# Spectral filter and gated layer on one core: the first stage's folded row in another layout, its last sums taken from VectorE to TensorE in ten of sixteen tiles

## Chip, core and metric

One NeuronCore of a Trainium2 chip runs one program. The time is that of the device for one execution, in microseconds; the kernel before took 716.36 us, the median of 3 runs (715.77 to 716.48). Lower is better.

## What is computed

`x` has 2048 rows (the sequence) of 640 features, in float32. Cut to what matters:

```python
h  = x + irfft2(rfft2(layernorm(x)) * (w_r + 1j * w_i))     # over both axes
z  = layernorm(h)
h2 = h + ((z @ w_gate) * (z @ w_up)) @ w_down               # 640 -> 1728 -> 640
```

`layernorm` takes the mean and the variance of each row, with no weights. All of the Fourier transforms are matrix products with tables of cosines and sines, which the host makes once.

## The kernel before

The 2048 rows lie in 16 tiles of 128 partitions. The forward transform along the rows is split in 128 x 16: **the first stage**, which is all that the change touches, multiplies each tile from the left with a 128x128 table `cct` of cosines and sines; the second stage then does the 640 features (`d_mm`), the other factor of the rows (`s2_mm`), the filter (`filt`), and the way back. After it come the second layernorm, and the gated layer as a long run of matrix products with the weights (a Strassen scheme in three passes of a rounded format).

In the first stage each tile is first *folded*, because a cosine is even about a point and a sine is odd: the 640 features become sums and differences of mirrored features, and half of the multiplications fall away. For tile `t`:

- **Statistics.** Mean and variance of the row. For some tiles VectorE does it (`bn_stats` twice, `bn_aggr`: L133, L134, L135), for those in `ON_ACT` ScalarE (two passes with an accumulator: L148, L149). Then the inverse root, for one, two or four tiles at a time: a square root on ScalarE (L158), and four tiny VectorE instructions, each of which needs the one before (L159 to L162). These four come in iterations 1, 5, 9 and 13 (and 3), zipped between the tile's fold instructions.
- **First fold.** `odd` subtracts mirrored features, for 2 x 160 outputs (L182; on GpSimd for tiles 0 to 6, on VectorE from tile 7 = `AHEAD` on). `even` adds them and takes twice the mean off, for 2 x 161 outputs (L192, one VectorE instruction).
- **Second fold**, within the same line of `even`: L196 adds the two halves for the 33 + 33 features for which TensorE will not do it, L197 subtracts them for 2 x 160.
- **Scaled table.** The inverse root belongs to the rows of the tile, which are summed over; so `scale_c` multiplies it into the table, `CR[t] = cct * r` (L214 on ScalarE for tile 0, L216 on VectorE for the others). Four buffers turn round.
- **Matrix products** (`s1_mm`). The folded tile is the stationary operand, the scaled table (128 columns) the moving one. Four blocks of 128 outputs go to one PSUM bank (`im`): the first two take two products each, over the two halves, so that TensorE does the sum of the second fold there (L208), the other two take one each, from the differences. The remaining 33 + 31 even and 64 odd features make one more product, into a bank of their own (L209). A float32 product is two hardware matmuls, so a tile is 14.
- **Out of PSUM.** ScalarE copies the four blocks (`s1_main`, L227) and the rest (`s1_rest`, L222). The bank of the four blocks has two buffers, so tile `t` waits for L227 of tile `t - 2`.

Each engine works off its own list in order. The order is written by hand: iteration `t` of the loop emits, for ScalarE, L222 of tile `t - 1`, its share of statistics, in some iterations the square root, L227 of tile `t - 1`; for VectorE, `odd` (from tile 7 on), the fold of tile `t` zipped with what `dve[t]` holds, its share of statistics, and the scaled table of tile `t + 1`; for TensorE, the products of tile `t`. Waits between instructions, also between two VectorE instructions of which one reads or overwrites what the other wrote, are put in by the framework, by the address range that each access spans.

After the last tile ScalarE copies its bank in two halves, `rest_split` (L231, L232) makes the rounded pairs, and `d_mm(0)` starts (L83, names `im<-tab,s` and `re<-tab,s`).

Of the kernel before, what the change touches and what calls it, by code (L numbers as in the profile page):

```python
# [14 lines left out]
OP = mybir.AluOpType  # L15

P = 128
S, D, NF, FF = 2048, 640, 321, 1728
NT = S // P
# [4 lines left out]
FOFF = (0, 160, 353, 514)  # L24
NR = 4
AHEAD = 7
ON_ACT = (1, 4, 10, 14)
EPS = 1e-5


def view(t, offset, dims):
    return bass.AP(tensor=t.tensor, offset=t.offset + offset, ap=[list(t.ap[0])] + [list(d) for d in dims])
# [6 lines left out]
def zipped(main, side):  # L39
    n = len(main)  # L40
    for i, f in enumerate(main):
        f()
        for h in side[i * len(side) // n:(i + 1) * len(side) // n]:
            h()
# [3 lines left out]
def tile_spectral_glu(ctx: ExitStack, tc: tile.TileContext, x, wf, wgu, wlast, wdown, wdlast,  # L48
                      cc, ci, fmain, frem, imain, irem, mm, out):
    nc = tc.nc  # L50
# [6 lines left out]
    tt, act = nc.vector.tensor_tensor, nc.scalar.activation  # L57
# [9 lines left out]
    def bank(tag, bufs=2):  # L67
        return pools["a"].tile([P, 512], F32, tag=tag, name=tag, bufs=bufs)
# [23 lines left out]
    XP = [keep.tile([P, D + 1], F32, name=f"x{t}") for t in range(NT)]  # L92
# [72 lines left out]
    SC = {}  # L165

    def front(ts):
        n = len(ts)
        r = small.tile([P, n], F32, tag="r", name="r")
        junk = [fold[:, o:o + D] for o in (NR * 1026, NR * 1026 + D)]  # L170
        m2, ve, fs = moments(ts, junk * 2 if ts[0] in ON_ACT else None)
        for i, t in enumerate(ts):
            SC[t] = r[:, i:i + 1], m2[:, i:i + 1]
        return fs, inverse_root(ve, r, n)

    def folded(t):
        o = t % NR * 1026
        return fold[:, o:o + 642], fold[:, o + 642:o + 1026]

    def odd(t, engine):  # L180
        f = folded(t)[0]
        engine.tensor_tensor(view(f, 0, [[160, 2], [1, 160]]), view(XP[t], 1, [[320, 2], [1, 160]]),  # L182
                             view(XP[t], 639, [[-320, 2], [-1, 160]]), op=OP.subtract)

    def even(t):
        f, j = folded(t)

        def both(n):
            return view(f, 0, [[320, 2], [1, n]]), view(f, 160, [[321, 2], [1, n]])

        return [
            lambda: nc.vector.scalar_tensor_tensor(view(f, 320, [[161, 2], [1, 161]]),  # L192
                                                   view(XP[t], 0, [[320, 2], [1, 161]]), SC[t][1],
                                                   view(XP[t], 640, [[-320, 2], [-1, 161]]),
                                                   op0=OP.subtract, op1=OP.add),
            lambda: tt(view(j, 33, [[-33, 2], [1, 33]]), *both(33), op=OP.add),  # L196
            lambda: tt(view(j, 64, [[1, 2], [2, 160]]), *both(160), op=OP.subtract),  # L197
        ]

    PS1, CR = {}, {}  # L200

    def s1_mm(t):
        pm, pr = PS1[t] = bank("im"), bank("ir2" if t % 2 else "im2", 1)
        (f, j), c = folded(t), CR[t]
        sums = [(f[:, o:o + P], f[:, o + n:o + n + P]) for o, n in ((31, 160), (353, 161))]
        for k, ls in enumerate((*sums, (view(j, 128, [[2, P]]),), (view(j, 129, [[2, P]]),))):
            for n, l in enumerate(ls):
                nc.tensor.matmul(pm[:, k * P:(k + 1) * P], l, c, start=n == 0, stop=n == len(ls) - 1)  # L208
        nc.tensor.matmul(pr[:, 0:P], j[:, 0:P], c, start=True, stop=True)  # L209

    def scale_c(t):
        CR[t] = crs[t % 4]
        if t == 0:
            act(CR[t], cct, AF.Copy, scale=SC[t][0])  # L214
        else:
            nc.vector.tensor_scalar(CR[t], cct, SC[t][0], None, op0=OP.mult)  # L216
# [4 lines left out]
    def s1_rest(t):  # L221
        act(at(rest, t), PS1[t][1][:, 0:P].rearrange("p (g m) -> p g m", g=32), AF.Copy)  # L222

    def s1_main(t):
        n = 4 if t < NT - 1 else 2
        for c in range(0, 4, n):
            act(view(s1, 4 * t + 2048 * c, [[2048, n], [64, 32], [1, 4]]),  # L227
                PS1[t][0][:, c * P:(c + n) * P].rearrange("p (c g m) -> p c g m", c=n, g=32), AF.Copy)
# [4 lines left out]

    banks("a", "pone")
    dve, acts, stats = ([[] for _ in range(NT)] for _ in range(3))
    post = {}

    warm = wk([P, P], "warm")
    nc.vector.memset(warm, 0.0)
# [7 lines left out]
    for first, n, a, b in ((2, 2, 0, 0), (4, 2, 0, 1), (6, 4, 1, 4), (10, 4, 2, 7), (14, 2, 8, 11)):  # L247
        fs, cs = front(range(first, first + n))
        if first in ON_ACT:
            for k, f in enumerate(fs[:-1]):  # L250
                acts[a + k * (b - a + 1) // (2 * n)].append(f)
            dve[b + 1].append(fs[-1])
        else:
            for k, f in enumerate(fs):
                stats[min(b, a + k // 3 * (b - a + 1) // n)].append(f)
        post[first - 2] = cs[0]
        dve[first - 1] += cs[1:]
    odd(0, nc.gpsimd)
    for t in range(NT):
        if t == 1:  # L260
            nc.gpsimd.dma_start(frt, frem)
        if t >= 1:
            s1_rest(t - 1)
            for f in acts[t]:
                f()
            if t >= AHEAD:
                odd(t, nc.vector)
            zipped(even(t), dve[t])
        else:
            e0 = even(0)  # L270
            for f in e0[:1] + c0 + e0[1:] + f1:
                f()
        if t + 2 < AHEAD:
            nc.gpsimd.tensor_copy(small.tile([P, 1], F32, tag="hold", name="hold"), folded(t)[1][:, 383:384])
            for k in (1, 2) if t == 0 else (t + 2,):
                odd(k, nc.gpsimd)
        if t >= 1:
            for f in stats[t]:
                f()
            if t in post:  # L280
                post[t]()
            s1_main(t - 1)
        else:
            scale_c(0)
            for f in c1[:1] + acts[0]:
                f()
            zipped(stats[0], c1[1:])
        if t + 1 < NT:
            scale_c(t + 1)
        if t == 0:  # L290
            post[t]()
        s1_mm(t)
    s1_main(NT - 1)
    s1_rest(NT - 1)
# [221 lines left out]
    def scale_shift(ts, junk, total=None):  # L516
        n = len(ts)
        r = small.tile([P, n], F32, tag="r", name="r")
        b = small.tile([P, n], F32, tag="b", name="b")
        m2, ve, fs = moments(ts, junk, total)  # L520
        cs = inverse_root(ve, r, n)
        cs.append(lambda: nc.vector.scalar_tensor_tensor(b, m2, -0.5, r, op0=OP.mult, op1=OP.mult))
        for i, t in enumerate(ts):
            SC[t] = r[:, i:i + 1], b[:, i:i + 1]
        return fs, cs
# [99 lines left out]
    for p in range(4):  # L625
        ts, t0 = (2 * p, 2 * p + 1), 2 * p + 2
        fs, cs = scale_shift(ts, [scrap] * 2, total[:, ts[0]:ts[0] + 2])
# [218 lines left out]
    for n, (blk, p) in enumerate(steps):  # L846
        if p == 6:
            s13, s12 = count % 3, (count + 1) % 3
            if blk == 0:
                load_raw(0)  # L850
                copies, sums, high, low = prep(0, blk, nc.vector)
# [26 lines left out]
            else:  # L878
                copies, sums, high, low = prep(0, blk)
# [41 lines left out]
            if blk == 0:  # L921
                fs, cs = scale_shift(range(8, 16), None)
# [5 lines left out]
        for ci in range(2):  # L928
            c = 2 * p + ci
# [28 lines left out]
def tables():  # L958
# [3 lines left out]
    for u in range(1, 64):  # L962
        a = 2 * np.pi * ((u * n2) % 128) / 128
# [12 lines left out]
    even = fr % 2 == 0  # L976

    def rows(kind, ds):
        r = np.zeros((len(ds), 2, NQ))
        for i, d in enumerate(ds):  # L980
            half = 0.5 if d == 160 or (d == 0 and kind[0] == "e") else 1.0
            if kind[0] == "e":
                r[i, 0, :NF] = np.where(even == (kind == "ee"), cs(fr, d) * half, 0)
            else:
                r[i, 1, :NF] = np.where(even == (kind == "oe"), -sn(fr, d) * half, 0)
        return r

    main = [rows(*a) for a in (("oe", np.arange(32, 160)), ("ee", np.arange(33, 161)),
                               ("os", np.arange(33, 161)), ("eo", np.arange(32, 160)))]
    cut = [(1, 0), (0, 0), (1, 160), (0, 160)]  # L990
    fmain = np.concatenate([a[:, b, o:o + w] for a, (b, o), w in zip(main, cut, FW)], 1)
    frem = np.concatenate([rows("ee", np.arange(33)), rows("oe", np.arange(1, 32)),
                           np.stack([rows("os", np.arange(1, 33)), rows("eo", np.arange(32))], 1).reshape(64, 2, NQ)])

    m = np.zeros((32, 128, 128), np.float64)
# [3 lines left out]
    for u in range(64):  # L999
        g, v = divmod(u, 2)  # L1000
        for pm in range(2):
            k = (u if pm == 0 else (128 - u if u else 64)) + 128 * r16
# [3 lines left out]
            for s in range(2):  # L1006
                pr = r16 * 4 + v * 2 + s
                if u == 0:
                    a = 1.0 if s == pm else 0.0
                else:  # L1010
                    a = 1.0 if s == 0 else (-1j if pm == 0 else 1j)
                w = (a * tw).T
# [4 lines left out]
                w = np.conj(a * tw) / (S * D)  # L1017
# [16 lines left out]
    for i, f in enumerate(fr):  # L1034
        a = 1.0 if f in (0, 320) else 2.0
        o = slice(0, 161) if f % 2 == 0 else slice(161, 322)
# [48 lines left out]
```

## Time and profile before

| | |
|---|---|
| median of 3 runs | 716.36 us |
| the profiled execution | 716.83 us |
| its span, first to last instruction | 715.0 us |
| TensorE clock granted | 0.999 |
| busy over the span: TensorE / VectorE / ScalarE / GpSimd | 98% / 65% / 36% / 40% |
| first stage: first VectorE work on a tile | 4.79 us |
| last tile's bank begins to leave PSUM | 44.08 us |
| first matmul of the second stage | 44.51 us |

How to read it: the profiled execution takes 1.83 us more than its span, and lies 0.47 us above the median. Lines are those of the kernel before. In the rows of a timeline the first number is the start in us from the beginning of the span, the second the duration of one instruction, or of a merged group from its first start to its last end; behind it stand engine, line, operation, out<-in, shapes and count, and in brackets how long the engine stood idle before and what ended that. PE is TensorE's matmuls, PEld its weight loads, DVE VectorE, ACT ScalarE, POOL GpSimd. The end of a matmul is modelled, and matmuls overlap, so their starts are what counts.

### The profile page before, as it was taken

What the parts mean: (1) busy time and instruction counts of PE and PEld (TensorE: products, weight loads), DVE (VectorE), ACT (ScalarE), POOL (GpSimd) and SP (SyncE); (2) the same over time, 40 slices, a digit from 0 to 9 for tenths busy, and PEclk for the clock granted to TensorE, in tenths of its full rate; (3) what the DMA queues carried; (4) which work ended last, traced back from release to release, by engine and by line L of the source; (5) the groups of instructions that cost most, each with busy time, mean ns of one, the idle gap of its engine ahead of it and who ended that gap; (6) DMA issues with size and microseconds to landing.
All of it is one profiled execution on the core that took longest, in us unless ns stands there. A gap on an engine that the chain in (4) does not pass through costs nothing.

```text
span 715.0 us, 10103 instructions
## 1 busy us (share of the span) xinstructions
PE 698.9 (98%) x3898; PEld 620.4 (87%) x3898; DVE 464.1 (65%) x808; ACT 254.6 (36%) x486; POOL 283.1 (40%) x263
## 2 busy tenths in 40 slices
PE   8899998999999999999999999999999999999998
PEld 7789998877788888989898989888888989898987
DVE  7978887897876656565555558565645555555454
ACT  6766665365532212222222255341222222222210
POOL 3101114331074645454554624055445355464600
PEclk9999999999999999999999999999999999999999
DMA  9406764000121212121211212301202121110203
GB/s 335 175 12 200 231 207 150 1 1 29 46 75 38 74 37 74 38 74 38 74 38 51 75 42 111 124 24 38 74 37 75 38 74 37 60 52 6 69 1 148
DMA packets 20928, 55.06 MB, mean 77 GB/s; under 512 B 2320, under 2 KB 6928, under 8 KB 20880
## 3 DMA queue, kind: packets, MB, share of 16 engines
q1 hardware_dynamic: 20304, 52.70, 21.3%
q0 software_dynamic: 288, 1.48, 0.6%
q8 instruction: 31, 0.51, 0.3%
q10 hardware_dynamic: 288, 0.23, 0.1%
q14 instruction: 17, 0.14, 0.1%
HBM read 49.16 MB, written 5.24 MB: 76 GB/s over the span
## 4 chain that ended last, share of the span: by engine, by line
PE 84%; DVE 11%; ACT 2%; issue 1%; DMA 1%; DVEq 0%; ACTq 0%
PE e L83 45%; PE y L83 27%; PE re L83 2%; PE im L83 2%; PE u L341 2%; PE eo L83 2%; PE im L383 1%; DVE x L512 1%; DVE fold L197 1%; DVE fold L192 1%; PE ir L383 1%; DMA raw<-in_wgu_dram 1%; ACT zt L529 1%; DVE x L514 1%; DMA x<-in_x_dram 1%
## 5 line engine op out<-in xcount | busy, mean ns | idle before, releaser
L83 PE MATMUL e<-xt,wst 128*128 128x512 f32 x864 | 206.8, 390 | 0.0
L83 PE MATMUL y<-wd,ht 128*128 128x320 f32 x1312 | 201.4, 310 | 1.2 <-DVE x L512 1.1
L83 PEld LDWEIGHTS y<-wd,ht 128*128 128x128 f32 x1312 | 195.3, 188 | 5.7 <-DVE x L512 2.7
L83 PEld LDWEIGHTS e<-xt,wst 128*128 128x128 f32 x864 | 160.7, 188 | 31.7
L512 DVE TENSOR_TENSOR x<-y,x 128x640 f32<-128x640 f32 x119 | 97.6, 821 | 70.4 <-PE y L83 70.1
L709 POOL TENSOR_TENSOR wst<-raw,wst 128x1024 fp32r<-128x1024 f32 x23 | 55.6, 2416 | 154.1 <-ACT wst L708 154.1
L725 POOL TENSOR_TENSOR wst<-raw,wst 128x896 fp32r<-128x896 f32 (+1 forms) x46 | 65.0, 1436 | 22.4 <-ACT wst L720 22.4
L468 POOL TENSOR_TENSOR wd<-draw,wd 128x640 fp32r<-128x640 f32 x28 | 44.9, 1627 | 72.1 <-ACT wd L467 72.1
L83 PE MATMUL e<-t,wst 128*128 128x512 f32 x288 | 73.2, 389 | 0.0
L821 ACT ACTIVATE ht<-e 128x512 fp32r<-128x512 f32 x24 | 14.4, 598 | 153.1 <-DVE e L820 153.1
L83 PEld LDWEIGHTS e<-t,wst 128*128 128x128 f32 x288 | 54.0, 188 | 11.7 <-DVE ht L660 0.5
L835 ACT ACTIVATE ht<-e 128x512 fp32r<-128x512 f32 x24 | 14.4, 598 | 114.0 <-DVE e L834 114.0
L83 PE MATMUL e<-xt,wdir 128*128 128x512 f32 x180 | 42.1, 392 | 1.2 <-DVE ht L664 1.2
L83 PEld LDWEIGHTS e<-xt,wdir 128*128 128x128 f32 x180 | 33.5, 188 | 8.6 <-ACT u L655 1.4
L708 ACT ACTIVATE wst<-raw 128x1024 fp32r<-128x1024 f32 x24 | 25.5, 1061 | 33.0 <-DMA raw<-in_wgu_dram 33.0
L413 POOL CAST qr<-bits 1x128 fp32r<-1x128 f32 x16 | 4.5, 280 | 82.4 <-DVE qr L408 81.5
L83 PE MATMUL e<-ht,wst 128*128 128x512 f32 x144 | 36.5, 389 | 0.0
L814 DVE TENSOR_TENSOR u<-e,u 128x512 f32<-128x512 f32 x24 | 16.6, 692 | 29.5 <-PE e L83 29.4
L208 PE MATMUL im<-bits,fold 128*128 128x128 f32 x192 | 27.9, 287 | 4.5 <-DVE bits L216 1.6
L83 PEld LDWEIGHTS e<-ht,wst 128*128 128x128 f32 x144 | 27.0, 188 | 5.6
L808 DVE TENSOR_TENSOR u<-e,p 128x512 f32<-128x512 f32 x24 | 16.6, 691 | 23.5 <-PE e L83 23.0
L720 ACT ACTIVATE wst<-raw 128x896 fp32r<-128x896 f32 (+1 forms) x48 | 30.0, 674 | 2.7 <-POOL raw L714 1.9
(183 smaller groups left out, 1019.0 us busy)
## 6 DMA issues: line engine op xcount, KB each, us to landing
raw<-in_wgu_dram SPq DMA_DIRECT2D x24, 640.0 KB, 3.9
wts<-in_wf_dram SPq DMA_DIRECT2D x16, 644.0 KB, 3.9
draw<-in_wdown_dram SPq DMA_DIRECT2D x24, 320.0 KB, 4.4
x<-in_x_dram SPq DMA_DIRECT2D x16, 320.5 KB, 6.0
out_dram<-x SPq DMA_DIRECT2D x15, 320.0 KB, 2.2
bits<-in_mm_dram SPq DMA_DIRECT2D x32, 128.0 KB, 3.9
raw<-in_wgu_dram SPq DMA_DIRECT2D x4, 320.0 KB, 4.3
draw<-in_wdlast_dram SPq DMA_DIRECT2D x4, 320.0 KB, 2.9
```

Source lines behind the costliest of these rows:

```text
L83: nc.tensor.matmul(o, l, r, start=start, stop=stop, skip_group_check=True)
L208: nc.tensor.matmul(pm[:, k * P:(k + 1) * P], l, c, start=n == 0, stop=n == len(ls) - 1)
L468: los.append(lambda r=r, a=a, b=b: engine.tensor_tensor(w[:, 1, a:b], r, f32(w[:, 0, a:b]), op=OP.subtract))
L512: tt(xv, ps[:, :, 0:320], xv, op=OP.add)
L708: act(wa[:, 0], stage[:, 0:1024], AF.Copy)
L709: ptt(wa[:, 1], stage[:, 0:1024], f32(wa[:, 0]), op=OP.subtract)
L720: act(ws[:, 0, o:o + b - a], stage[:, a:b], AF.Copy)
L725: ptt(ws[:, 1, o:o + b - a], stage[:, a:b], f32(ws[:, 0, o:o + b - a]), op=OP.subtract)
L808: tt(u2, o6, p1, op=OP.add)
L814: tt(u2, o5, u2, op=OP.add)
L821: act(hh[1], o3, AF.Copy)
L835: act(hh[0], o4, AF.Copy)
```

## The change

The folded row is laid out anew. Before, the 2 x 160 odd values stood first and the 2 x 161 even ones behind; now each half is a block of 321, even values first. The even block that TensorE sums now takes features 0 to 127, so that the remaining 33 even and 31 odd values stand next to each other (columns 128 to 191 of a half). With that, their sum is one contiguous VectorE instruction of 64 values (new L194), or, for the tiles in `SUM_ON_PE`, two TensorE products of 64 columns that add up in PSUM, with a third of 64 columns for the remaining differences, instead of one of 128: 18 hardware matmuls in place of 14. The three write partitions 0 to 63 and 64 to 127 of the rest's bank. In the built program they carry an array tile of 128x64, all other products, also those of 65 columns at L383, one of 128x128. The host's tables follow the new order; their sizes stay.

From tile 7 on, the scaled table of tile `t + 1` is made by VectorE directly behind the even fold of tile `t`, in place of after the second fold; not in the iterations that hold the four instructions of the root, and for tiles 13, 14 and 15 ScalarE makes it, behind L227.

Because `odd` and `even` now write interleaved blocks, the address ranges that they span overlap: in the changed program each even fold waits for the odd one (VectorE's own, or GpSimd's for tiles 0 to 6). L196 and L197 also overlapped before, in two columns; the new L194 and L195 do not, and L195 no longer waits for it. The first product of a tile now reads columns within the span of the even fold, and waits for it; before, it needed only the odd one.

```diff
+SUM_ON_PE = (0, 1, 2, 3, 4, 5, 6, 9, 13, 15)
+SCALE_ON_ACT = (0, 13, 14, 15)
 ...
     def odd(t, engine):
         f = folded(t)[0]
-        engine.tensor_tensor(view(f, 0, [[160, 2], [1, 160]]), view(XP[t], 1, [[320, 2], [1, 160]]),
+        engine.tensor_tensor(view(f, 161, [[321, 2], [1, 160]]), view(XP[t], 1, [[320, 2], [1, 160]]),
                              view(XP[t], 639, [[-320, 2], [-1, 160]]), op=OP.subtract)
     def even(t):
         f, j = folded(t)
 ...
-            lambda: nc.vector.scalar_tensor_tensor(view(f, 320, [[161, 2], [1, 161]]),
 ...
-            lambda: tt(view(j, 33, [[-33, 2], [1, 33]]), *both(33), op=OP.add),
-            lambda: tt(view(j, 64, [[1, 2], [2, 160]]), *both(160), op=OP.subtract),
+        fs = [lambda: nc.vector.scalar_tensor_tensor(view(f, 0, [[321, 2], [1, 161]]),
 ...
+        if t not in SUM_ON_PE:
+            fs.append(lambda: tt(j[:, 0:64], f[:, 128:192], f[:, 449:513], op=OP.add))
+        fs.append(lambda: tt(view(j, 64, [[1, 2], [2, 160]]), view(f, 161, [[-161, 2], [1, 160]]),
+                             view(f, 482, [[-161, 2], [1, 160]]), op=OP.subtract))
+        return fs
 ...
     def s1_mm(t):
         pm, pr = PS1[t] = bank("im"), bank("ir2" if t % 2 else "im2", 1)
         (f, j), c = folded(t), CR[t]
-        sums = [(f[:, o:o + P], f[:, o + n:o + n + P]) for o, n in ((31, 160), (353, 161))]
-        for k, ls in enumerate((*sums, (view(j, 128, [[2, P]]),), (view(j, 129, [[2, P]]),))):
+        both = lambda o, w: (f[:, o:o + w], f[:, 321 + o:321 + o + w])
+        parts = [(pm[:, k * P:(k + 1) * P], ls)
+                 for k, ls in enumerate((both(192, P), both(0, P), (view(j, 128, [[2, P]]),), (view(j, 129, [[2, P]]),)))]
+        if t in SUM_ON_PE:
+            parts.insert(2, (pr[0:64, 0:P], both(P, 64)))
+            parts.append((pr[64:128, 0:P], (j[:, 64:128],)))
+        else:
+            parts.append((pr[:, 0:P], (j[:, 0:P],)))
+        for o, ls in parts:
             for n, l in enumerate(ls):
-                nc.tensor.matmul(pm[:, k * P:(k + 1) * P], l, c, start=n == 0, stop=n == len(ls) - 1)
-        nc.tensor.matmul(pr[:, 0:P], j[:, 0:P], c, start=True, stop=True)
+                nc.tensor.matmul(o, l, c, start=n == 0, stop=n == len(ls) - 1)
     def scale_c(t):
         CR[t] = crs[t % 4]
-        if t == 0:
+        if t in SCALE_ON_ACT:
             act(CR[t], cct, AF.Copy, scale=SC[t][0])
 ...
+        roots.add(first - 1)
 ...
+            fs = even(t)
             if t >= AHEAD:
                 odd(t, nc.vector)
-            zipped(even(t), dve[t])
+                if t + 1 < NT and t + 1 not in SCALE_ON_ACT and t not in roots:
+                    fs.insert(1, lambda: scale_c(t + 1))
+            zipped(fs, dve[t])
 ...
-        if t + 1 < NT:
+        if t + 1 < NT and (t < AHEAD or t + 1 in SCALE_ON_ACT or t in roots):
             scale_c(t + 1)
```

In the host's tables, `main` and `frem` take the even rows 0 to 127 and 128 to 160 in place of 33 to 160 and 0 to 32.

More of the change, by code (lines that the diff above doesn't have):

```diff
@@ L186, in even @@
         f, j = folded(t)
[L188 to L198, printed above, removed]
+        fs = [lambda: nc.vector.scalar_tensor_tensor(view(f, 0, [[321, 2], [1, 161]]),
+                                                     view(XP[t], 0, [[320, 2], [1, 161]]), SC[t][1],
+                                                     view(XP[t], 640, [[-320, 2], [-1, 161]]),
+                                                     op0=OP.subtract, op1=OP.add)]
+        if t not in SUM_ON_PE:
[3 more added lines that the diff above has]
+        return fs
     PS1, CR = {}, {}
@@ L235, in tile_spectral_glu @@
     dve, acts, stats = ([[] for _ in range(NT)] for _ in range(3))
-    post = {}
+    post, roots = {}, set()
     warm = wk([P, P], "warm")
@@ L986, in rows @@
         return r
-    main = [rows(*a) for a in (("oe", np.arange(32, 160)), ("ee", np.arange(33, 161)),
+    main = [rows(*a) for a in (("oe", np.arange(32, 160)), ("ee", np.arange(128)),
                                ("os", np.arange(33, 161)), ("eo", np.arange(32, 160)))]
@@ L991, in tables @@
     fmain = np.concatenate([a[:, b, o:o + w] for a, (b, o), w in zip(main, cut, FW)], 1)
-    frem = np.concatenate([rows("ee", np.arange(33)), rows("oe", np.arange(1, 32)),
+    frem = np.concatenate([rows("ee", np.arange(128, 161)), rows("oe", np.arange(1, 32)),
                            np.stack([rows("os", np.arange(1, 33)), rows("eo", np.arange(32))], 1).reshape(64, 2, NQ)])
```

## The prediction

> **What bounds the kernel now.** The busy time by stretch, cut where the first stage takes up work, changes its order (tile 7) and ends, and one stretch after it:
>
> ```profile
> core 0: us, PE busy (x) PEld busy (x) DVE busy (x) ACT busy (x) POOL busy (x), PEclk, DMA share, GB/s
> 5.00:25.50 20.50, 16.51 (x119) 14.78 (x118) 19.25 (x77) 14.91 (x42) 7.19 (x13) 1.00 1.05 395
> 25.50:43.30 17.80, 17.27 (x133) 15.72 (x133) 16.98 (x55) 11.94 (x33) 0.00 (x0) 1.00 0.03 9
> 60.00:110.00 50.00, 50.00 (x340) 46.30 (x339) 41.96 (x57) 33.28 (x79) 8.62 (x23) 1.00 0.64 212
> ```
>
> The 98% of TensorE say nothing of the first stage. There VectorE is busy for 19.25 of 20.5 us and then 16.98 of 17.8. TensorE's 17.27 is modelled ends that overlap: 133 matmuls in 17.8 us are one each 0.134 us, against 0.112 when dense (below). From 60 us on TensorE has no gap, so whatever the first stage ends earlier, the whole kernel does. The hand-over:
>
> ```profile
> 44.08 0.66 ACT L227 ACTIVATE s<-im 128x256 f32<-128x256 f32 x2 [0.86 <-PE im L208]
> ```
> ```profile
> 44.51 0.40 PE L83 MATMUL im<-tab,s 128*128 128x160 f32 x1 [0.25 <-ACT s L227]
> ```
>
> ScalarE copies the last bank at 44.08, held up by TensorE, and the second stage follows. So I forecast that 44.08.
>
> **VectorE, tiles 0 to 6.** The sum L196 goes from all seven. Tiles 0, 1 and 2:
>
> ```profile
> 7.53 0.49 DVE L197 TENSOR_TENSOR fold<-fold 128x320 f32<-128x320 f32 x1
> 8.11 0.15 DVE L151 TENSOR_SCALAR ve<-sq 128x1 f32<-128x1 f32 x1
> ```
> ```profile
> 11.61 0.16 DVE L159 RECIPROCAL r<-sd 128x2 f32<-128x2 f32 x1
> 11.79 0.23 DVE L196 TENSOR_TENSOR fold<-fold 128x66 f32<-128x66 f32 x1
> 11.94 0.15 DVE L160 SCALAR_TENSOR_TENSOR w<-r 128x2 f32<-128x2 f32 x1
> ```
> ```profile
> 13.92 0.55 DVE L192 SCALAR_TENSOR_TENSOR fold<-x,m 128x322 f32<-128x322 f32 x1
> 14.57 0.23 DVE L196 TENSOR_TENSOR fold<-fold 128x66 f32<-128x66 f32 x1
> 14.83 0.49 DVE L197 TENSOR_TENSOR fold<-fold 128x320 f32<-128x320 f32 x1
> ```
>
> In tile 0 VectorE then waits for ScalarE (L197 to L151 is 0.58, elsewhere L197 to the next is 0.41): no gain. In tile 1 L196 holds 11.79 to 11.94, 0.15; so in 3 and 5, which also have the root. In tile 2 L192 to L197 is 0.91; without L196 it is L192's 0.55 and 0.03 for the wait, 0.58: 0.33; so in 4 and 6. Sum 3 x 0.15 + 3 x 0.33 = **1.44**.
>
> **VectorE, tiles 7 to 15.** Tile 12, and the end of tile 9's root:
>
> ```profile
> 35.22 0.28 DVE L216 TENSOR_SCALAR bits<-cct,r 128x128 f32<-128x128 f32 x1
> 35.41 0.49 DVE L182 TENSOR_TENSOR fold<-x 128x320 f32<-128x320 f32 x1
> 35.81 0.55 DVE L192 SCALAR_TENSOR_TENSOR fold<-x,m 128x322 f32<-128x322 f32 x1
> 36.40 0.23 DVE L196 TENSOR_TENSOR fold<-fold 128x66 f32<-128x66 f32 x1
> 36.66 0.49 DVE L197 TENSOR_TENSOR fold<-fold 128x320 f32<-128x320 f32 x1
> 37.07 0.16 DVE L151 TENSOR_SCALAR ve<-sq 128x2 f32<-128x2 f32 x1
> ```
> ```profile
> 25.61 0.49 DVE L182 TENSOR_TENSOR fold<-x 128x320 f32<-128x320 f32 x1
> ```
> ```profile
> 29.79 0.55 DVE L192 SCALAR_TENSOR_TENSOR fold<-x,m 128x322 f32<-128x322 f32 x1
> 30.25 0.17 DVE L159 RECIPROCAL r<-sd 128x4 f32<-128x4 f32 x1
> 30.37 0.23 DVE L196 TENSOR_TENSOR fold<-fold 128x66 f32<-128x66 f32 x1
> 30.52 0.15 DVE L160 SCALAR_TENSOR_TENSOR w<-r 128x4 f32<-128x4 f32 x1
> ```
> ```profile
> 31.70 0.48 DVE L182 TENSOR_TENSOR fold<-x 128x320 f32<-128x320 f32 x1
> ```
>
> The row at 37.07 is what follows the tile. A tile takes 37.07 - 35.22 = 1.85: L216 0.19, L182 0.40, L192 0.59, L196 0.26, L197 0.41. An instruction that waits for the one before pays its full duration and some 0.03; one that doesn't starts earlier: L192 to L159 is 0.46 against 0.59 to L196, and L196 to L160 is 0.15 against 0.26 to L197.
>
> After: L182 to the even fold is a wait now, 0.49 + 0.03 = 0.51 instead of 0.40 (**the change costs 0.11 here**); then the scaled table after 0.46, 0.20 for it, by when the fold is done; the sum 0.15, now free of L197's wait; the difference 0.41. Together 1.73, 0.12 less. (The Trainium skill, page "VectorE: DVE Perf Modes", section "The DRAIN you can't avoid", says that a semaphore between Vector instructions costs nothing extra. By that the new wait would cost nothing and such a tile would take 1.62. The trace disagrees: 0.15 against 0.26 behind the same L196.) Where ScalarE makes the table, tile 12: 0.51 + 0.58 + 0.15 + 0.41 = 1.65, and 0.07 for L151. In tile 9 the root's second step waited behind L196; it gains only 0.08, and the wait takes 0.11.
>
> Two edits I cost at nothing. ScalarE's tables for tiles 13 to 15 fall into its idle time (0.86 us even ahead of the last copy) and are due a tile later; if they come late, one of them, some 0.3 to 0.4 by the other copies' rows, lies on TensorE's path. And the even fold's wait for GpSimd's odd one:
>
> ```profile
> 12.76 0.85 POOL L182 TENSOR_TENSOR fold<-x 128x320 f32<-128x320 f32 x1
> ```
> ```profile
> 16.50 0.55 DVE L192 SCALAR_TENSOR_TENSOR fold<-x,m 128x322 f32<-128x322 f32 x1
> ```
>
> GpSimd works two tiles ahead: tile 3's odd fold is done at 13.61, its even fold starts at 16.50. Behind the waiting fold stand the rest of VectorE's list and TensorE's products; a tile's margin of 2.9 us must go before that matters.
>
> **TensorE.** Dense loads first, then the restart behind a wait and how long one load and one matmul are given (least, middle and most ns), then 65-column weights:
>
> ```profile
> 38.01 0.97 PEld L208 LDWEIGHTS im<-bits,fold 128*128 128x128 f32 x8
> ```
> ```profile
> 43.30 0.50 PE L208 MATMUL im<-bits,fold 128*128 128x128 f32 x2
> ```
> ```profile
> L208 PEld LDWEIGHTS im<-bits,fold x192: 186/192/199, 9.1 to 43.6; 128*128 128x128 f32 x192
> L208 PE MATMUL im<-bits,fold x192: 275/275/387, 9.2 to 43.8; 128*128 128x128 f32 x192
> ```
> ```profile
> 55.79 0.50 PEld L383 LDWEIGHTS ir<-bits,y 128*65 128x65 f32 x4
> 56.27 0.97 PEld L383 LDWEIGHTS im<-bits,y 128*128 128x128 f32 x8
> ```
>
> Each matmul has its load; 8 loads in 0.97, the last taking 0.192, are 0.111 apart. I use 0.112. After a wait the second comes 0.50 - 0.275 = 0.22 behind the first: 0.11 lost. Four loads of 65 columns take 0.48, no less per piece, so I give a 64-column product 0.112 too. A tile on TensorE then takes 18 x 0.112 = 2.02 instead of 1.57. That is the price, and it makes TensorE late:
>
> ```profile
> 19.28 0.55 DVE L192 SCALAR_TENSOR_TENSOR fold<-x,m 128x322 f32<-128x322 f32 x1
> ```
> ```profile
> 22.62 0.27 ACT L222 ACTIVATE rest<-im 128x128 f32<-128x128 f32 x1
> ```
> ```profile
> 24.47 0.57 ACT L227 ACTIVATE s<-im 128x512 f32<-128x512 f32 x1
> ```
> ```profile
> 28.60 0.28 ACT L222 ACTIVATE rest<-ir 128x128 f32<-128x128 f32 x1
> ```
> ```profile
> 29.49 0.19 ACT L158 ACTIVATE sd<-ve 128x4 f32<-128x4 f32 x1
> ```
>
> - Tile 4: even fold 19.28 - 0.63 (tiles 1 to 3) = 18.65, done 19.23; TensorE 19.28 + 0.11 + 2.02 = 21.41; ScalarE's L222 0.2 later (0.275 - 0.112, and 0.04) and 0.06 behind the copy that stands ahead of it, 21.67; from there to the end of L227 it is 24.47 + 0.57 - 22.62 = 2.42, so tile 6 gets its bank at 24.15.
> - Tile 6: 24.15 + 0.11 + 2.02 = 26.28. Tile 7: + 1.57 = 27.85. Its L222 comes 0.2 later, 28.05; to the end of the square root 29.49 + 0.19 - 28.60 = 1.08: 29.13.
> - VectorE would be ready for tile 9's root at 25.61 - 1.44 + 1.73 + 1.80 + 0.51 + 0.46 = 28.67. It waits to 29.19: **0.52 given back**.
> - From there to the next L182: 31.70 - 30.25 - 0.08 = 1.37, so 30.56. Tiles 10, 11, 12: 1.73, 1.73, 1.72: 35.74. Tile 13's even fold is done 0.51 + 0.58 later, 36.83.
> - TensorE: tile 13 36.88 + 0.11 + 2.02 = 39.01; tile 14 + 1.57 = 40.58; tile 15's four blocks 16 x 0.112 = 1.79. The last of these starts at 42.26; with 0.275 and 0.04 ScalarE copies at **42.57**.
>
> 44.08 - 42.57 = 1.51 less. The span becomes 713.5, the profiled execution 716.83 - 1.51 = 715.3; it lies 0.47 above the median, so the median becomes 716.36 - 1.51 = **714.9**. Working out every engine in this way for the kernel before leaves me some 0.3 off its rows, and the early waits are the weakest part: 714.2 to 715.5.
>
> **Rivals.**
>
> *1. The 64-column products stop the array (slower).* Each tile in the set goes from 128-wide array tiles to 64-wide ones and back twice: four switches, 40 in all. No row of before has one; the 65-column loads next to 128-column ones (55.79 to 56.27 to the next) show no gap, but these carry the full array tile. A gap's price: 0.11, the restart, if only the load comes late; 0.275 - 0.112 = 0.16 if a matmul must have left the array; both, 0.27. At 0.16 a tile is 2.67 and TensorE, from tile 0 on at 9.1, has no slack left: tiles 0 to 6 18.7 (27.8), 7 and 8 3.1, 9 2.7, 10 to 12 4.7, 13 2.7, 14 1.6, the last 1.8 + 0.5 + 0.2, and some 0.5 for the banks: 45.6, 1.5 later, **717.9**. At 0.11 it is about 716.6, at 0.27 about 721. It decides from about 0.1 on, where the gain is gone. For it: 40 switches at 0.16 are 6.4 us on an engine that my sum has as the last one late. Against it: no row does. (The Trainium skill, "TensorEngine Tiling (Array Packing)", section "Tiling Modes", says: "Mode switching requires drain: Changing tiling mode (not just tile) drains the TensorE". It gives no time. By that rule this rival is the case; no run here shows it yet.)
>
> *2. TensorE and ScalarE do not hold VectorE up.* Without the 0.52 the end comes at 42.05, and with 64-column products 0.01 shorter than I take them (12 in tile 15 and 13) at 41.9: 2.2 less, **714.2**. For it: nothing but VectorE and the root's 1.45 us sets tile 9 in the rows of before, where ScalarE's square root was done at 29.68, half a microsecond ahead. Against it: TensorE's 18 matmuls a tile.
>
> *3. The change does not shorten the first stage.* Waits that I cost at nothing (the even fold on GpSimd's odd one, two waits at one instruction, ScalarE's tables, a switch of 0.05 to 0.1) eat it up: **716.3**. For it: L192 to L196 is 0.65 in tile 2, with a wait for GpSimd, against 0.59 in tile 12. Against it: each alone is under 0.1 a tile.
>
> **How the numbers follow.** My forecast 0.45, rival 1 0.25, rival 2 0.15, rival 3 0.15. What a measurement here can tell from no change is about 0.2%, 1.43 us: under 714.93 is faster, over 717.79 slower. Of my forecast a little over half lies under it, 0.26, and all of rival 2, 0.15: 0.41. Slower is the part of rival 1 with a switch of 0.16 or more, 0.18. The rest, 0.41, is within. The range takes in the forecast and rivals 2 and 3 and rival 1 up to a switch of about 0.17: 713.9 to 718.4; above it stays the dear part of rival 1, about 0.1, below it less.
>
> **What would show it.** Right: L196's slots gone from tiles 0 to 6; L182 to even fold 0.51 from tile 7 on; 18 matmuls in about 2.0 us, with loads still 0.11 apart around the 64-column ones; VectorE idle about half a microsecond at tile 9's L159, TensorE dense from tile 13 to the end; the copy of the last bank at 42.6. Wrong: gaps of 0.1 or more on both sides of each 64-column product (rival 1), no wait at tile 9 (rival 2), new idle time of VectorE in tiles 1 to 6 (rival 3).

## The result and the profile after

The changed kernel takes **717.55 us** (median of 17 runs, 717.31 to 718.0), the kernel before on the same chip 715.84 (17 runs): the ratio is 1.0022 with an interval of 1.0014 to 1.0029, a loss of 1.71 us where I forecast a gain of 1.5. The span grew from 715.0 to 715.7. ScalarE's copy of the last bank, forecast for 42.57, starts at 45.78 instead of 44.08. These 1.70 us agree with the 1.71 of the medians, so the question stays in the first stage. (The spans say less: from that copy to its end the profiled execution of the kernel before takes 715.0 - 44.08 = 670.9 us, the changed kernel's 715.7 - 45.78 = 669.9, and all the runs below between 669.8 and 670.2.)

The same two stretches of the changed kernel, columns as before:

```profile
5.00:25.50 20.50, 20.50 (x144) 16.92 (x143) 19.21 (x75) 15.04 (x42) 7.10 (x13) 1.00 1.05 397
25.50:43.30 17.80, 17.77 (x135) 15.64 (x135) 14.27 (x44) 12.12 (x34) 0.00 (x0) 1.00 0.02 8
```

The bound has changed its engine. TensorE's busy time in the first stretch went from 16.51 to 20.50 of 20.50, and VectorE's in the second fell from 16.98 to 14.27. But TensorE issued only 144 matmuls in those 20.5 us, one in 0.142, so it is busy without being dense (a busy time is made of modelled ends). VectorE's rows (L184 is the odd fold, L189 the even one, L194 the sum, L195 the difference, L221 the table, L153 and L161 the statistics and the root's first step):

```profile
24.00 0.48 DVE L184 TENSOR_TENSOR fold<-x 128x320 f32<-128x320 f32 x1
24.51 0.56 DVE L189 SCALAR_TENSOR_TENSOR fold<-x,m 128x322 f32<-128x322 f32 x1
24.99 0.28 DVE L221 TENSOR_SCALAR bits<-cct,r 128x128 f32<-128x128 f32 x1
25.18 0.22 DVE L194 TENSOR_TENSOR fold<-fold 128x64 f32<-128x64 f32 x1
25.32 0.48 DVE L195 TENSOR_TENSOR fold<-fold 128x320 f32<-128x320 f32 x1
25.72 0.48 DVE L184 TENSOR_TENSOR fold<-x 128x320 f32<-128x320 f32 x1
...
28.93 0.17 DVE L153 TENSOR_SCALAR ve<-sq 128x4 f32<-128x4 f32 x1 [1.41 <-ACT fold L151]
...
30.72 0.18 DVE L161 RECIPROCAL r<-sd 128x4 f32<-128x4 f32 x1 [0.63 <-ACT sd L160]
```
```profile
42.09 0.49 DVE L195 TENSOR_TENSOR fold<-fold 128x320 f32<-128x320 f32 x1
```

Up to tile 7 VectorE does what was forecast and more: it begins tile 7 at 24.00 instead of 25.61, 1.61 early (forecast 1.44), and tile 7 takes 25.72 - 24.00 = 1.72 (forecast 1.73). Then it stands idle twice in tile 9, 1.41 + 0.63 = 2.04 us. What it waits for, on ScalarE:

```profile
27.82 0.28 ACT L227 ACTIVATE rest<-im 128x128 f32<-128x128 f32 x1 [1.23 <-PE im L214]
27.99 0.82 ACT L151 ACTIVATE fold<-x,m 128x640 f32<-128x640 f32 x1
28.71 0.19 ACT L151 ACTIVATION_READ_ACCUMULATOR fold<-x,m 128x1 f32 x1
```
```profile
45.78 0.66 ACT L232 ACTIVATE s<-im 128x256 f32<-128x256 f32 x2 [1.38 <-PE im L214]
```

The statistics L151 stand in ScalarE's queue behind the copy L227 of a remainder bank, and that copy waited 1.23 us for TensorE. So TensorE is late, ScalarE's in-order queue hands its lateness to VectorE, and at the end VectorE has long been done (42.09) when TensorE's last bank comes. TensorE's rows from tile 13's sum product (`128*64`, four matmuls) to tile 15's:

```profile
40.13 0.65 PE L214 MATMUL ir<-bits,fold 128*64 128x128 f32 x4
40.71 0.74 PE L214 MATMUL im<-bits,fold 128*128 128x128 f32 x4
41.38 0.43 PE L214 MATMUL ir<-bits,fold 128*64 128x128 f32 x2
41.74 2.75 PE L214 MATMUL im<-bits,fold 128*128 128x128 f32 x22
44.42 0.65 PE L214 MATMUL ir<-bits,fold 128*64 128x128 f32 x4
```

No row names a wait, and yet each of the four stretches between crossings is too long. Four narrow matmuls at 0.112 are 0.45, and the next row starts 0.58 later: 0.13 too much. Four wide ones, again 0.45, take 0.67 up to the next narrow: 0.22 too much. Two narrow ones, 0.22, take 0.36: 0.14 too much. The last 22 wide ones, 2.46, take 2.68: 0.22 too much. From 40.13 to 44.42 there are 32 matmuls, 3.58 us at 0.112; the 4.29 leave 0.71 for four switches. That is rival 1's picture: gaps on both sides of the 64-column products. The view of the product line says the same: its first entry under idle time is issue, time in which TensorE waited for nothing that the profile shows (us, times):

```profile
  issue: 1.7, 10
```

### The profile page after: what moved, and what is told of

It is laid out like the page before. It is cut to its first block, busy times and chain, and to the rows that moved or that the text cites. A ratio compares the mean times of both kernels' runs of the same rounds, so it can differ in the third digit from the quotient of the medians.

```text
span 715.7 us, 10168 instructions
## 1 busy us (share of the span) xinstructions
PE 705.3 (99%) x3938; PEld 623.9 (87%) x3938; DVE 461.1 (64%) x795; ACT 255.7 (36%) x489; POOL 283.1 (40%) x263
## 4 chain that ended last, share of the span: by engine, by line
PE 88%; DVE 8%; ACT 2%; issue 1%; DVEq 0%; ACTq 0%
PE e L85 43%; PE y L85 27%; PE im L214 4%; PE re L85 2%; PE im L85 2%; PE u L350 2%; PE eo L85 2%; PE im L392 2%; PE re L247 1%; DVE x L521 1%; PE ir L392 1%; PE ir L214 1%; ACT zt L538 1%; DVE x L523 1%; DVE q L506 1%
## 5 line engine op out<-in xcount | busy, mean ns | idle before, releaser
L214 PE MATMUL im<-bits,fold 128*128 128x128 f32 (+1 forms) x224 | 32.0, 289 | 0.0
L214 PEld LDWEIGHTS im<-bits,fold 128*128 128x128 f32 (+1 forms) x224 | 26.9, 187 | 4.7 <-issue 1.7
```

The source lines that it names most:

```text
L214: nc.tensor.matmul(o, l, c, start=n == 0, stop=n == len(ls) - 1)
```

## The experiments

Theory S: what the sum lacked is the switch between 128- and 64-column array tiles, some 0.16 to 0.18 us each, four to a tile. Rivals: 18 matmuls a tile are too many even without switches; the new layout or the tables' places cost the time; the further work on ScalarE does. Medians below stand beside the kernel before on the same chip: 716.03 for e1 to e4, 715.77 for e5 to e8, 716.18 for e9 to e12.

**No switch (e6).** All products 128 columns wide, the same 18 matmuls, one copy:

```diff
-            parts.insert(2, (pr[0:64, 0:P], both(P, 64)))
-            parts.append((pr[64:128, 0:P], (j[:, 64:128],)))
+            parts.insert(2, (pr[:, 0:P], both(P, P)))
+            parts.append((pr[:, P:2 * P], (j[:, 64:64 + P],)))
```

This kernel leaves out the right upper 64 rows of the rest: the one copy takes them from the sum product.

> All products 128 columns wide as in the third run, but one ScalarE copy a tile: the upper 64 remainder rows come from the sum product instead of the last one, whose result is left unread, so this kernel leaves out the right place of those rows and only its time counts. Theory: with no switch and no further copy the prediction's sum holds, 18 matmuls in 2.02 us, the last copy at 42.3 to 42.9 and the time 1.2 to 1.8 us under before (714.0 to 714.7); the third run's 43.80 was the second copy, 0.17 us on each of ten tiles on the engine that hands the banks back. Rival: 18 matmuls a tile are too many for TensorE even without a switch, because the three on-TensorE tiles 4 to 6 and the waits for tables and banks stand behind each other; then it stays near the third run, 715.4 to 715.9.

Measured: 714.06 (ratio 0.9974, interval 0.9964 to 0.9983). From the timelines of this kernel, tile 13's sum (its own name is `ir` here too, now 128 wide) and tile 15's, VectorE's wait in tile 9, and the last copy:

```profile
37.73 0.61 PE L214 MATMUL ir<-bits,fold 128*128 128x128 f32 x4
38.18 0.64 PE L214 MATMUL im<-bits,fold 128*128 128x128 f32 x4
38.65 0.39 PE L214 MATMUL ir<-bits,fold 128*128 128x128 f32 x2
38.87 2.69 PE L214 MATMUL im<-bits,fold 128*128 128x128 f32 x22
41.40 0.61 PE L214 MATMUL ir<-bits,fold 128*128 128x128 f32 x4
```
```profile
29.00 0.18 DVE L161 RECIPROCAL r<-sd 128x4 f32<-128x4 f32 x1 [0.44 <-ACT sd L160]
```
```profile
42.51 0.66 ACT L233 ACTIVATE s<-im 128x256 f32<-128x256 f32 x2 [1.08 <-PE im L214]
```

The same 32 matmuls take 41.40 - 37.73 = 3.67 us, 0.62 less than in the changed kernel. The prediction's sum comes out almost to the row: the root at 29.00 after a wait of 0.44 (29.19 and 0.52 there), the last copy at 42.51 (42.57 there). The rival that 18 matmuls are too many falls.

**Six switches (e9).** The changed kernel, with one wide product between the two halves of the sum product:

```diff
+        steps = [(o, l, n == 0, n == len(ls) - 1) for o, ls in parts for n, l in enumerate(ls)]
+        if t in SUM_ON_PE:
+            steps.insert(6, steps.pop(5))
 ...
```

> The changed kernel with its products in another order: the two halves of the sum product of the ten tiles are set apart by one 128-column product, so that a tile has three narrow stretches instead of two, six switches instead of four; the products, waits and results are the same. Theory: each switch stops the array for 0.17 us and the ten tiles are bound by TensorE, so 20 more switches cost up to 3.4 us: last copy at 48.3 to 49.2, 2.5 to 3.4 us over the changed kernel's 717.55, 720.0 to 721.0. Rival: what the changed kernel lost is not in the switches but in how the narrow products or their bank hold up the rest; then the order matters little, 717.0 to 718.2.

Measured: 720.69 (ratio 1.0068, interval 1.0052 to 1.0083). The same stretch of TensorE, from tile 13's sum to tile 15's, and the last copy:

```profile
42.56 0.43 PE L216 MATMUL ir<-bits,fold 128*64 128x128 f32 x2
42.93 0.50 PE L216 MATMUL im<-bits,fold 128*128 128x128 f32 x2
43.36 0.43 PE L216 MATMUL ir<-bits,fold 128*64 128x128 f32 x2
43.72 0.50 PE L216 MATMUL im<-bits,fold 128*128 128x128 f32 x2
44.16 0.43 PE L216 MATMUL ir<-bits,fold 128*64 128x128 f32 x2
44.52 2.75 PE L216 MATMUL im<-bits,fold 128*128 128x128 f32 x22
47.20 0.43 PE L216 MATMUL ir<-bits,fold 128*64 128x128 f32 x2
```
```profile
48.90 0.66 ACT L234 ACTIVATE s<-im 128x256 f32<-128x256 f32 x2 [1.72 <-PE im L216]
```

32 matmuls with 0, 4 and 6 switches: 3.67, 4.29 and 4.64 us, so **0.16 to 0.18 us a switch**. 20 more of them moved the last copy by 48.90 - 45.78 = 3.12, and by 3.1 the time: in the changed kernel TensorE has nothing left in which a switch could hide. It is the order alone that costs this.

**Two switches (e2, e7).** In e2 the sum product goes to the tile's end, next to the other narrow one. In e7 that other one is written to the same 64 columns of the array besides (and the copy in these ten tiles takes 64 rows alone, with the other 64 rows of the rest, which this kernel leaves out, set to zero by GpSimd at 0.74 us, before the first stage):

```diff
-            parts.insert(2, (pr[0:64, 0:P], both(P, 64)))
+            parts.append((pr[0:64, 0:P], both(P, 64)))
-            parts.append((pr[64:128, 0:P], (j[:, 64:128],)))          # e7
+            parts.append((pr[0:64, P:2 * P], (j[:, 64:128],)))        # e7
```

> The same 18 products a tile as the changed kernel, but the three of 64 columns stand together at the tile's end: two switches between array tiles of 128 and of 64 columns in place of four. If each switch costs 0.17 us, a tile of the ten takes 2.36 us instead of 2.70, and the kernel is 0.5 to 1.0 us faster than before (2.2 to 2.7 faster than the changed one). If the cost lies in the number of products or in the narrow products themselves, it stays 1.3 to 1.8 us slower than before.

> The second run's kernel (the three 64-column products together at the tile's end, two switches a tile), but the last of them is written to the same 64 columns of the array as the two before it, beside them in the bank; the ScalarE copy of these ten tiles takes the lower 64 rows alone, so the upper 64 remainder rows are left out. Theory: two narrow products run at one time only if they sit in different halves of the columns. Then the pairs of starts 0.013 us apart go, six narrow matmuls take 0.65 us instead of 0.43, the tile grows by 0.22 us, and over the tiles that TensorE bounds the kernel is 0.3 to 1.3 us longer than the second run: 714.2 to 715.2. Rival: the pairs come from narrow products following one another, whatever their half; then the starts keep 0.013 us and the time stays at 713.7 to 714.1.

Measured: e2 713.92 (0.9964, 0.9951 to 0.9976), last copy at 42.12, 2.1 us under before, more than I had expected. e7 714.92 (0.9988, 0.9979 to 0.9997), last copy at 42.92. The copies, e2 and then e7:

```profile
42.12 0.66 ACT L232 ACTIVATE s<-im 128x256 f32<-128x256 f32 x2 [0.60 <-PE im L214]
```
```profile
42.92 0.66 ACT L234 ACTIVATE s<-im 128x256 f32<-128x256 f32 x2 [0.60 <-PE im L215]
```

Tile 9's narrow products and the next wide one, e2 and then e7:

```profile
31.03 0.65 PE L214 MATMUL ir<-bits,fold 128*64 128x128 f32 x6
31.61 3.31 PE L214 MATMUL im<-bits,fold 128*128 128x128 f32 x26
```
```profile
31.39 0.87 PE L215 MATMUL ir<-bits,fold 128*64 128x128 f32 x6
32.19 3.26 PE L215 MATMUL im<-bits,fold 128*128 128x128 f32 x26
```

The six narrow matmuls hold TensorE for 0.58 us in e2 and 0.80 in e7; the 0.22 between them is two matmuls. The window from 31.00 to 31.06 in e2 holds the first two of the six narrow matmuls; the second line has the durations of all six (least, middle and most ns):

```profile
31.03 0.34 PE L214 MATMUL ir<-bits,fold 128*64 128x128 f32 x2
```
```profile
L214 PE MATMUL ir<-bits,fold x6: 272/273/323, 31.0 to 31.4; 128*64 128x128 f32 x6
```

The two together last 0.34 us and each of them at least 0.272, so they start at most 0.07 us apart, where dense ones are 0.11 apart. (By the program's order the first two would both be the sum's, in one half. The rows don't name the product; that the last product starts beside the sum's is argued from e7, where the overlap is gone.) So narrow products run side by side if they sit in different halves, and that is worth 42.92 - 42.12 = 0.80 us of what e2 got beyond the expectation. The other 45.78 - 42.92 = 2.86 us against the changed kernel are the two switches a tile that are gone, and in tile 15 the narrow products that now stand behind the bank that ends the stage; no run separates these two. The changed kernel has the two halves' products apart, with four wide matmuls between, and pays both ways.

**Two narrow products in the kernel before (e4).**

```diff
-        nc.tensor.matmul(pr[:, 0:P], j[:, 0:P], c, start=True, stop=True)
+        for h in (0, 64):
+            nc.tensor.matmul(pr[h:h + 64, 0:P], j[:, h:h + 64], c, start=True, stop=True)
```

> The kernel before, with the one product of the rest (L209) split into two of 64 columns, for partitions 0 to 63 and 64 to 127: 16 matmuls a tile and two switches a tile, nothing else changed. If a switch costs 0.17 us, a tile takes 1.57 + 0.22 + 0.34 = 2.1 us on TensorE, more than VectorE's 1.85, and the kernel gets 1.5 to 2.5 us slower. If switches are free, 1.8 us a tile hide behind VectorE: 0 to 0.2 us slower.

Measured: 715.89 (0.9994, 0.9985 to 1.0003), last copy at 44.23 against 44.08: no difference in the time. The first case of the expectation missed; the number of the second came, but not by its reason, as switches aren't free here either.

```profile
32.53 0.44 PE L210 MATMUL ir<-bits,fold 128*64 128x128 f32 x4
32.90 1.64 PE L208 MATMUL im<-bits,fold 128*128 128x128 f32 x12
34.46 0.44 PE L210 MATMUL im<-bits,fold 128*64 128x128 f32 x4
```

Its four narrow matmuls take 32.90 - 32.53 = 0.37 up to the next wide one; the changed kernel's two take 0.36. So the second product was free: it ran beside the first, and the 0.22 that the expectation gave it was the error. A tile of TensorE is 34.46 - 32.53 = 1.93 us, 14 slots of 0.112 and 0.36 for two switches, and VectorE's tile is 1.85; with the waits that the kernel before has anyway that all but hides. A switch costs the kernel time only where TensorE is the bound.

**All wide, with a second copy (e3).** As e6, but the correct rows are fetched by another ScalarE instruction in each of the ten tiles:

```diff
+            for h in range(2):
+                act(at(rest[64 * h:64 * h + 64], t), pr[0:64, h * P:h * P + P].rearrange("p (g m) -> p g m", g=32), AF.Copy)
```

> The same 18 products a tile, but the three narrow ones take 128 columns (64 of them of no use) and write two column ranges of the rest's bank, which ScalarE then copies in two pieces of 64 partitions, one copy of some 0.17 us more a tile. No switch is left. If the switches are the cost: 0.11 us a matmul, 2.04 us a tile, 0.6 to 1.2 us faster than before. If it is the number of products: as slow as the changed kernel, or slower by the copies.

Measured: 715.77 (0.9995, 0.9986 to 1.0004), last copy at 43.80: no gain that can be told from none, against the expected 0.6 to 1.2. The copies, and for the product line L214 what TensorE waited for, in e3 and then in e6 (us, times):

```profile
40.18 0.55 ACT L230 ACTIVATE rest<-ir 64x128 f32<-64x128 f32 x2 [0.98 <-PE ir L214]
```
```profile
  ACT s L237: 5.0, 10
```
```profile
  ACT s L233: 1.0, 4
```

The pair takes 0.55 where one copy takes 0.28 (0.27 more, where I had expected 0.17), and ScalarE hands the main banks back late: TensorE stood idle for them for 5.0 us instead of 1.0. The copies are all that e3 and e6 differ in, and 43.80 - 42.51 = 1.29 us is their price. I had taken ScalarE's idle time for room enough.

**The other parts (e1, e5).** e1 leaves every sum on VectorE; e5 also puts the tables back where they stood:

```diff
-SUM_ON_PE = (0, 1, 2, 3, 4, 5, 6, 9, 13, 15)
+SUM_ON_PE = ()
-SCALE_ON_ACT = (0, 13, 14, 15)                                   # e5
+SCALE_ON_ACT = (0,)                                              # e5
 ...
-                if t + 1 < NT and t + 1 not in SCALE_ON_ACT and t not in roots:
-                    fs.insert(1, lambda: scale_c(t + 1))         # e5
 ...
-        if t + 1 < NT and (t < AHEAD or t + 1 in SCALE_ON_ACT or t in roots):
+        if t + 1 < NT:                                           # e5
```

> The changed kernel with no tile's sum on TensorE: 14 products a tile, all of 128 columns; the new layout and the moved tables stay. If the narrow products are what makes the change slow (by their switches or by their number), this is faster than before by 1.2 to 1.8 us, the last bank's copy at about 42.6 instead of 44.08. If the new layout's waits are at fault (even fold on the odd one, TensorE's first product on the even fold), it is slower than before or the same.

> The changed kernel with only its first part: the new layout of the folded row, with no sum on TensorE, and the scaled tables back where they stood, on VectorE behind the difference (tile 0's on ScalarE). Theory: by rows already measured a steady tile is odd fold 0.52, even fold 0.58 with the wait for its result, sum 0.15, difference 0.41, table 0.20 = 1.86 us against 1.85 before, so tiles 7 to 15 gain nothing; tiles 0 to 6 lose the wait between sum and difference, 0.26 to 0.15, at most 7 x 0.11 = 0.8. So 0.3 to 0.9 us faster than before, and the last copy at 43.2 to 43.8; the other 0.9 to 1.5 of the 1.77 us of the kernel without sums on TensorE come from the tables' places. Rival: the layout alone carries all of it, 714.2 to 714.6; then the places of the tables are worth nothing.

Measured: e1 714.26 (0.9969, 0.9956 to 0.9981), last copy at 42.44; e5 715.44 (0.9997, 0.9988 to 1.0005), last copy at 43.64. The copies, e1 and then e5:

```profile
42.44 0.66 ACT L232 ACTIVATE s<-im 128x256 f32<-128x256 f32 x2 [0.73 <-PE im L214]
```
```profile
43.64 0.66 ACT L232 ACTIVATE s<-im 128x256 f32<-128x256 f32 x2 [0.85 <-PE im L214]
```

By these rows the layout alone gives 44.08 - 43.64 = 0.44 and the tables' places 43.64 - 42.44 = 1.20; the times show the two together, but e5's alone can't be told from no change. In the changed kernel the sums on TensorE, in the order in which they stand, cost 45.78 - 42.44 = 3.34.

Beside e6 this says more: with the ten sums on TensorE and no switch at all the last copy starts at 42.51, without any of them at 42.44. So the ten sums, moved in this way, bring nothing even without a switch, and the gain that the forecast gave them is there without them. VectorE begins tile 7 at 23.96 in e6 and 24.69 in e1, 0.73 ahead; behind the wait in tile 9 it begins tile 10 at 30.36 and 30.61, 0.25 ahead; and tile 15 has four matmuls more on TensorE ahead of its last bank, 0.45.

**A better version (e8, e10, e11, e12).** e2's order, with the sums on TensorE only in the tiles where VectorE has statistics besides its folds:

```diff
-SUM_ON_PE = (0, 1, 2, 3, 4, 5, 6, 9, 13, 15)
+SUM_ON_PE = (0, 1, 2, 3, 4, 5)                                   # e8; e10: and 9; e11: and 15; e12: without 5
```

> The second run's kernel with the sum on TensorE in tiles 0 to 5 alone, where VectorE has the statistics and the folds beside it, instead of in ten tiles. Theory: in tiles 6 to 15 TensorE with 2.1 us a tile is slower than VectorE with 1.73, so those sums are worth more on VectorE: 0.3 to 0.9 us under the second run, 713.0 to 713.6, last copy at 41.2 to 41.9. Rival: the sums of tiles 6, 9, 13 and 15 fall where VectorE has extra work (a root, an odd table) and TensorE has time; without them it is no better, 713.8 to 714.3.

> The eighth run's kernel with tile 9 on TensorE besides tiles 0 to 5: tile 9 stands with a root on VectorE that costs it about 0.5 us, so TensorE has time there. Theory: the sum's 0.15 us on VectorE goes and nothing comes in its place, 713.2 to 713.4. Rival: VectorE waits for ScalarE's root in that tile anyway, or TensorE's 2.1 us come back at tile 10: 713.4 to 713.7.

> The eighth run's kernel with the last tile on TensorE besides tiles 0 to 5: the sum of tile 15 leaves VectorE 0.15 us ahead of its last difference, and the narrow products stand behind the bank that ends the stage. Theory: 0.1 to 0.2 us under the eighth run, 713.2 to 713.4. Rival: the last bank waits for TensorE and not for the difference, so it is the same or a switch later, 713.4 to 713.8.

> The eighth run's kernel with tiles 0 to 4 on TensorE only. Theory: VectorE bounds the tiles up to 6, so tile 5's sum is worth there what the others are, and without it the kernel is 0.1 to 0.2 us longer, 713.5 to 713.7. Rival: TensorE comes out of the first six tiles late, with 2.1 us for each, and gains by one tile less: 713.1 to 713.4.

Measured: e8 **713.43** (0.9967, 0.9955 to 0.998), 2.3 us under before. Its last copy:

```profile
41.58 0.66 ACT L232 ACTIVATE s<-im 128x256 f32<-128x256 f32 x2 [0.73 <-PE im L214]
```

That is 0.54 earlier than in e2, and the medians say 0.5 as well; the ratios, measured on two chips, don't tell e2 and e8 apart. e10 713.36 (0.9963, 0.9951 to 0.9976), e11 713.48 (0.9965, 0.9952 to 0.9977) and e12 713.45 (0.9964, 0.9952 to 0.9977), with last copies at 41.60, 41.81 and 41.62: all four lie within 0.12 us, and which of them is best stays open. In e11 the copy comes 0.2 later, as its rival said; e12's expected loss of 0.1 to 0.2 doesn't show. Against e1, which has no sum on TensorE, e8's copy is 42.44 - 41.58 = 0.86 earlier. So the idea holds in the first tiles, where VectorE is the bound, and in tiles 9 and 15 it buys nothing that these runs can tell; tiles 6 and 13 weren't tried one by one.

## Why the prediction was wrong

**The step that failed** is TensorE's price of a tile: "so I give a 64-column product 0.112 too. A tile on TensorE then takes 18 x 0.112 = 2.02 instead of 1.57", with nothing for the switch. Dense, the 18 cost almost that (32 matmuls in 3.67 in e6, 2.06 for 18); what was missing is four switches of 0.16 to 0.18, some 0.7 us on each of ten tiles. All of it together is 40 x 0.165 = 6.6 us. The first and last starts of the product line show what became of it, in e6 and in the changed kernel:

```profile
L214 PE MATMUL im<-bits,fold x224: 275/275/378, 8.5 to 42.2; 128*128 128x128 f32 x112
L214 PE MATMUL ir<-bits,fold x40: 275/275/275, 12.6 to 42.4; 128*128 128x128 f32 x40
```
```profile
L214 PE MATMUL im<-bits,fold x224: 272/275/387, 8.8 to 45.5; 128*128 128x128 f32 x100, 128*64 128x128 f32 x12
L214 PE MATMUL ir<-bits,fold x40: 272/273/324, 12.6 to 45.8; 128*64 128x128 f32 x36, 128*128 128x128 f32 x4
```

264 matmuls in both, from 8.5 to 42.4 (33.9 us) and from 8.8 to 45.8 (37.0). At 0.112 they are 29.6: in e6 this leaves 4.3 us in which TensorE stood, in the changed kernel, with 6.6 for the switches, 0.8. So by this count, an estimate, 3.5 us of the switches went into idle time that TensorE had, and the other 3.1 into the end. Of those waits e6's view of the line names these two first; in the changed kernel's the first has shrunk to the last line and the second is gone (us, times):

```profile
  DVE fold L189: 1.9, 2
  ACT rest L228: 1.2, 3
```
```profile
  DVE fold L189: 0.2, 1
```

All waits that the two views name, without issue, are 4.3 us in e6 and 1.8 in the changed kernel: 2.5 us less, so the 3.5 may be too high.

The evidence that I took for "no switch" was no evidence: the 65-column loads next to wide ones keep the full array tile, as the prediction itself said under rival 1. No row of before had a switch, so the price had to be bounded and the sum made for its middle, not for nothing. **Rival 1** was worked out with 0.16, came to 45.6 and 717.9, and the chip gave 45.78 and 717.55: mechanism, place and price were right, its chance of 0.25 too low for what the prediction itself set down for it, 40 switches on the engine that its sum has as the last one late. (The Trainium skill, "TensorEngine Tiling (Array Packing)", section "Tiling Modes", says that a change of mode drains TensorE, and that different tiles run loads and matmuls in parallel. The trace agrees with both: 0.16 to 0.18 us a switch, and 0.22 us less for six narrow matmuls on both halves than on one. I gave this too little weight.)

The other steps, by the rows:

- L196's slots in tiles 0 to 6: 1.44 forecast, 1.61 measured at tile 7. Tiles 1, 2, 4, 5 and 6 came as forecast (0.17 to 0.34 each); tile 0 gave 0.26 where nothing was expected and tile 3 nothing where 0.15 was, so the sum is a little better than its parts. Of the 1.61 the layout brings 0.92 without any sum moved: e1 begins tile 7 at 24.69 instead of 25.61.
- The odd-to-even wait: 0.51 forecast, 24.51 - 24.00 = 0.51. Right. A steady tile 1.73, measured 1.72. Right.
- VectorE waiting for TensorE at tile 9: 0.52 forecast, 0.44 in e6, where there are no switches; 2.04 with them; none in e1, with 14 matmuls a tile. The mechanism was right, the size hung on the failed step.
- The even fold's wait for GpSimd: taken as nothing, and rightly. In the changed kernel GpSimd's odd fold of tile 3 is done at 13.17 and the even one starts at 15.73; in tile 6 it is 20.64 and 22.81.
- ScalarE's tables for tiles 13 to 15: taken as nothing. e1 has them, with its last copy at 42.44. They weren't tried one by one.
- **Rival 2** (TensorE doesn't hold VectorE up) is wrong: even e6 waits 0.44. **Rival 3** named a switch of 0.05 to 0.1 among its causes; the place was right, the price too low.
- Two flaws of the working that change no conclusion: at each hand-over from one engine to the next the sum adds 0.05 to 0.06 that it doesn't name (19.23 to 19.28, 24.09 to 24.15, 29.13 to 29.19, 36.83 to 36.88). And rival 1's other two prices don't follow from its own terms: with the same 39 switches up to the last copy, 0.27 gives about 722 and not 721, and 0.11 about 715.8 and not 716.6.

## What to carry to other kernels

Price a product by the array tile it runs on, not by its columns alone: every change between 128- and 64-column products stops TensorE, so put narrow products together, opposite halves next to each other, and count the changes left. An operation moved off a bounding engine is worth its time only where the engine that takes it has slack; move it in those stretches and leave it elsewhere. Where no row shows what an edit adds, and the engine that it lands on is the last one late, the sum should carry the middle of the bounds and not zero.

## What the runs showed of the hardware

- A switch of the array tile costs 0.16 to 0.18 us for float32 matmuls of 128 columns (3.67, 4.29 and 4.64 us for 32 matmuls with 0, 4 and 6), in both directions: the stretches above, of narrow and of wide ones, are each 0.13 to 0.22 too long.
- Two 64-column products in different halves of the array run at once: in e4 four narrow matmuls took 0.37 us to the next wide one, where two alone took 0.36. In the same half they don't (e7: 0.80 for six against 0.58).
- A ScalarE copy of 64 partitions takes as long as one of 128 (both of 128 columns): in e3 0.55 for two of 64 against 0.28 for one of 128.
